# A tuned FFT-filter and MLP kernel: a last FFT stage without a turn through DRAM, and a first batch made in two copies

## The chip, the cores and the metric

The kernel runs on one core of a Trainium2 chip. The metric is the device time of one execution in microseconds (us). Each kernel was timed in rounds beside the kernel before on the same chip. The class of a result is "same" when it lies within 2%.

## The reference, cut to what matters

```python
# x: (8, 3008, 256); filt: (1505, 256); w_in: (256, 2048); w_out: (2048, 256)
X = np.fft.rfft(x, axis=1)
Y = X * (filt_r + 1j * filt_i)[None]
y = np.fft.irfft(Y, n=3008, axis=1)
t = y.reshape(24064, 256)
h = t @ w_in
out = (h * (1 / (1 + np.exp(-beta * h)))) @ w_out
```

So each of eight batches is filtered in the frequency domain along its 3008 rows, and every row then goes through an MLP with 2048 hidden values.

## The kernel before

The FFT is done as matmuls in four stages: first stage (`s1`), second and third stage with the filter product between them (`s23`), last stage (`s4`). Between the stages the data change their layout. From the second batch on that is done through DRAM: `d1` between the first and second stage, `d2` between the third and the last, and a third exchange `dy` with a transposing read, since the MLP wants channels on the partitions. A copy of a matmul's result out of the accumulators (PSUM) into SBUF, by VectorE or ScalarE, is called an eviction here. The names in the profile are `a` and `d` (or `d_931`) for the first exchange, `z`, `d` (or `d_932`) and `zz` for the second, `yo`, `dy`, `y` for the third.

The MLP goes in steps: one block of 512 rows and one slice of 128 hidden values is one step. Sixteen steps are a block, 752 steps the whole. The FFT units of later batches are put between MLP steps by a table, `plan`:

```python
def s4(b, i, on_act):                      # last stage, 16 units per batch
    ...
    nc.tensor.matmul(ps[:KP], lhsT=t4[:], rhs=s["zz"][g][:, jj : jj + 2, :], ...)  # table stationary
    evac(s["yo"][...], ps[...], on_act, inv_scale)
    if jj + 2 == JG:
        nc.sync.dma_start(s["dyr"][...], s["yo"]...)          # y to DRAM
def y_read(b):
    for c in range(NDC):
        nc.sync.dma_start_transpose(ys[b][:, c, :S], s["dy"][c, :S, :])   # and back, turned
...
place(w_, 0.00, 0.14, u1(b, True))         # batch 1 (the second): first stage at steps 0 to 13
place(w_, 0.28, 0.60, u23(b), True)
...
place(w_, 0.03, 0.48, u23(b), True)        # later batches; parts of a window of 96 steps
```

`u1(b, True)` lets every other eviction of the first stage go to ScalarE, and `True` in `place` ("clear") keeps a unit off the steps whose number modulo 16 is 0, 1, 14 or 15, where VectorE copies the output block `ost` out.

The first batch has no MLP to hide behind. Its stages run first, on chip, with transposes. There the filter's imaginary part is loaded once to 64 partitions, negated into the other 64 by GpSimd (`copy_imag`), and four rounds of transposes (`turn`) and last-stage matmuls (`last`) make all of y before the first MLP step.

## Time and profile before

The median is 845.16 us of three runs (844.58 to 845.36). I cut each execution at two points: the first MLP matmul ("start"), and the first MLP step that needs batch 1 (step 80). The rest is the time from there to the end of the span.

| kernel before, profiled run | us |
|---|---|
| span | 844.1 |
| first MLP matmul | 66.6 |
| first 80 steps | 111.5, of it TensorE busy 91.8 |
| step 80 to the end | 666.0 |
| period of a batch in the steady part | 96.26 |

The mark for step 80 is 178.09, after the waits of 4.6 us for the turned y that fall inside that step. In the other kernels the mark is that step's first matmul, so here about half a microsecond of the step's work counts with the first 80 that counts with the rest elsewhere. This is the windows view of the first 80 steps (stretch, length, busy time of PE, PEld, DVE, ACT and POOL with instruction counts, granted clock, DMA share, GB/s; PE is TensorE's matmuls, PEld its weight loads, DVE VectorE, ACT ScalarE, POOL GpSimd, SPq SyncE's queue, and the granted clock is the share of full speed that TensorE was given), and then the SyncE's issues in it (start, us, what):

```profile
66.60:178.09 111.49, 91.76 (x562) 59.07 (x573) 46.29 (x68) 72.45 (x117) 23.51 (x28) 0.91 0.66 160
```

```profile
85.99 0.30 SPq L496 DMA_DIRECT2D d_931<-a_1078  x1
91.56 0.38 SPq L507 DMA_DIRECT2D a_1131<-d_931  x1
...
132.52 0.36 SPq L554 DMA_DIRECT2D d_932<-z  x1
139.61 2.43 SPq L561 DMA_DIRECT2D zz<-d_932  x4
```

### The profile page before, as it was taken

To read this page: it belongs to the slowest core of one execution; us is meant where nothing else is said; L and a number is where in the kernel's file an instruction comes from. 1 tells how busy PE (TensorE), PEld (TensorE's weight loads), DVE (VectorE), ACT (ScalarE), POOL (GpSimd) and SP (SyncE) were. 2 spreads that over 40 slices of the span, in tenths; PEclk is the share of its full clock that TensorE was granted. 3 is DMA by queue.
4 is the path that set the end of the run, shared out by engine and by line. 5 is a ranking of instruction groups with operands and counts; after the bars stand their busy time and mean duration, and the time that the engine had idled before them with its cause. 6 is when DMAs were issued, how large, how long until landed. Compare 5 with 4: busy or idle time off the path is not lost.

```text
span 844.1 us, 14640 instructions
## 1 busy us (share of the span) xinstructions
PE 797.0 (94%) x5634; PEld 553.8 (66%) x5723; DVE 410.9 (49%) x638; ACT 602.0 (71%) x911; POOL 179.9 (21%) x189
## 2 busy tenths in 40 slices
PE   7589886979999999999999999999999999999997
PEld 4476564657666776677666876677666776666665
DVE  7643483326563575627564475636565463510101
ACT  5627576748867787678866787678866788677775
POOL 5792242013210241003310232003300131000000
PEclk9778998889999999999999999999999999999999
DMA  8574627852198134951289323961266423550101
GB/s 167 117 164 84 164 82 179 262 99 64 47 275 230 57 106 110 310 146 47 61 216 267 83 89 100 280 188 61 63 194 186 113 64 92 151 142 26 52 26 50
DMA packets 132280, 110.06 MB, mean 130 GB/s; under 512 B 47009, under 2 KB 117682, under 8 KB 132210
## 3 DMA queue, kind: packets, MB, share of 16 engines
q1 hardware_dynamic: 127570, 95.74, 39.8%
q0 software_dynamic: 4640, 13.37, 9.2%
q8 instruction: 45, 0.74, 0.4%
q14 instruction: 25, 0.20, 0.1%
HBM read 54.01 MB, written 57.67 MB: 132 GB/s over the span
## 4 chain that ended last, share of the span: by engine, by line
PE 85%; DMA 7%; issue 3%; DVE 2%; POOL 2%; SPq 1%; ACT 1%; DVEq 0%; POOLq 0%; ACTq 0%
PE acc L693 38%; PE hps L665 35%; DMA fi_sb<-in_filt_i_dram 2%; PE pz L424 1%; DVE ost L705 1%; POOL fi_sb L138 1%; DMA zz<-d_932 1%; DMA xg<-in_x_dram 1%; DMA dy<-yo 1%; DMA y<-dy 1%; DMA d_931<-a_1078 1%; DMA a_3015<-d_2714 1%; DMA a_6777<-d_6476 0%; DMA a_1131<-d_931 0%; DVE q_t L529 0%
## 5 line engine op out<-in xcount | busy, mean ns | idle before, releaser
L674 ACT ACTIVATE gT<-hps,beta_sb 128x512 bf16<-128x512 f32 x752 | 516.1, 687 | 193.4 <-PE hps L665 171.4
L693 PE MATMUL acc<-wout_sb,gT 128*128 128x256 bf16 x3008 | 457.5, 274 | 3.8
L665 PE MATMUL hps<-y,win_sb 128*128 128x512 bf16 (+7 forms) x1643 | 433.6, 353 | 5.1 <-DMA y<-dy 4.6
L693 PEld LDWEIGHTS <-gT 128*128 128x128 bf16 x3008 | 293.6, 98 | 163.3 <-issue 7.6
L535 POOL TENSOR_TENSOR v_t<-p_t,q_t 128x512 bf16<-128x512 f32 x84 | 106.5, 1268 | 407.0 <-DVE q_t L529 348.2
L665 PEld LDWEIGHTS <-win_sb 128*128 128x128 bf16 x1728 | 166.1, 98 | 28.8 <-issue 4.9
L705 DVE COPY ost<-acc 128x512 f32<-128x512 f32 x94 | 60.4, 683 | 214.5 <-PE acc L693 214.1
L113 POOL DMA_DIRECT2D xg<-in_x_dram x32 | 17.2, 537 | 101.6 <-PE ps_4036 L491 8.8
L517 PEld LDWEIGHTS <-t_102 128*128 128x128 bf16 x168 | 16.0, 98 | 19.3 <-issue 4.6
L570 PEld LDWEIGHTS <-t_101 96*96 96x96 bf16 x112 | 14.0, 126 | 21.6 <-DMA zz<-d_932 8.2
L491 PEld LDWEIGHTS <-t_100 94*96 94x96 bf16 x112 | 14.0, 125 | 13.5 <-issue 0.9
L545 PEld LDWEIGHTS <-t_103 128*128 128x128 bf16 x168 | 16.0, 98 | 8.4 <-issue 3.1
L114 POOL DMA_DIRECT2D xg<-in_x_dram x32 | 16.4, 513 | 0.0
L138 POOL TENSOR_SCALAR fi_sb<-fi_sb 64x1536 f32<-64x1536 f32 x4 | 16.3, 4100 | 0.1
L395 PE MATMUL psz<-t3q,qb_t 128*128 128x128 bf16 x48 | 7.9, 244 | 8.3 <-DVE qb_t L386 7.7
L184 PE MATMUL pw<-wz 128*128 128x512 bf16 x37 | 14.2, 477 | 1.2 <-DVE wz L178 1.2
L149 POOL TENSOR_SCALAR wout_sb<-ws,rbeta_sb 128x256 bf16<-128x256 f32 x16 | 14.5, 940 | 1.3 <-DMA ws<-in_moe_w_out_dram 1.3
L99 ACT ACTIVATE z_t<-psz 128x512 bf16<-128x512 f32 x12 | 7.1, 597 | 8.8 <-PE psz L395 8.7
L395 PEld LDWEIGHTS <-qb_t 128*128 128x128 bf16 x48 | 5.1, 110 | 10.3 <-DVE qb_t L386 10.1
L424 PE MATMUL pz<-ident,z_t 128*96 128x128 bf16 x64 | 11.2, 353 | 0.5 <-ACT z_t L99 0.5
L424 PEld LDWEIGHTS <-z_t 128*96 128x96 bf16 x64 | 10.8, 257 | 0.8 <-ACT z_t L99 0.8
L101 DVE COPY zz<-pz 96x1024 bf16<-96x1024 bf16 x8 | 5.5, 687 | 9.8 <-PE pz L424 9.8
(1026 smaller groups left out, 661.3 us busy)
## 6 DMA issues: line engine op xcount, KB each, us to landing
out_dram<-ost SPq DMA_DIRECT2D x47, 512.0 KB, 3.0
dy<-yo SPq DMA_DIRECT2D x28, 384.0 KB, 5.0
xg<-in_x_dram POOLq DMA_DIRECT2D x32, 320.0 KB, 6.5
ws<-in_moe_w_out_dram SPq DMA_DIRECT2D x4, 512.0 KB, 6.6
xg<-in_x_dram POOLq DMA_DIRECT2D x32, 56.0 KB, 6.7
fr_sb<-in_filt_r_dram SPq DMA_DIRECT2D x8, 192.0 KB, 6.7
fi_sb<-in_filt_i_dram SPq DMA_DIRECT2D x8, 192.0 KB, 7.3
d_932<-z SPq DMA_DIRECT2D x4, 384.0 KB, 3.8
```

The lines of the kernel that those rows point to most:

```text
L113: nc.gpsimd.dma_start(t[:80], xv[:80, js, :])
L114: nc.gpsimd.dma_start(t[80:NP], xv[80:NP, js, :])
L138: eng.tensor_scalar_mul(fi_sb[M:P, ks_, :], fi_sb[:M, ks_, :], -1.0)
L149: nc.gpsimd.tensor_scalar_mul(wout_sb[:, f0 + i, :], ws[:, i, :], rbeta_sb[:, f0 + i : f0 + i + 1])
L424: nc.tensor.transpose(pz[:KP, e, dc * P : (dc + 1) * P], z_t[:, dc, :, JG * g + 4 * i + e], ident[:],)
L517: nc.tensor.matmul(ps[:, e, :], lhsT=t2[:, k0 + e, :, :].rearrange("p c k -> p (c k)"), rhs=s["a2"][g][:, kk + e, :], start=True, stop=True,)
L535: nc.gpsimd.tensor_tensor(v_t[:], p_t[:], q_t[:], ALU.add)
L545: nc.tensor.matmul(ps[:, e, :], lhsT=t3[:, k0 + e, :, :].rearrange("p c k -> p (c k)"), rhs=v_t[:, e, :], start=True, stop=True,)
L665: nc.tensor.matmul(hps[:, pos - t0 : pos - t0 + ln], lhsT=win_sb[:, dc, fb * P : (fb + 1) * P], rhs=ys[b][:, dc, n0 : n0 + ln], start=(dc ...
L674: nc.scalar.activation(gT[:, :tn], hps[:, :tn], ACT.Silu, scale=beta_sb[:, fb : fb + 1])
L693: nc.tensor.matmul(acc[tb // 2][:, tb % 2, :], lhsT=gT[:, tb * P : (tb + 1) * P], rhs=wout_sb[:, fb, :], start=(fb == 0 and tb % 2 == 0), ...
L705: nc.vector.tensor_copy(ost[:, 2 * h : 2 * h + n, :], acc[h][:, :n, :])
```

## The change

Its intent is threefold. The last stage takes the data as the stationary side in all batches, so that y comes out with channels on the partitions and needs no third exchange. The first batch's spectrum is made twice, with the filters loaded to both halves of the partitions, so that no negation and no copies stand in the start (the later batches still need the negated filter; GpSimd makes it after the start, from 66 us on). And of the first batch's last stage only the first of four classes of rows is made before the MLP; three are placed within the first 50 steps, in a row order that `store` undoes.

The core of the diff, cut (`...`):

```diff
 def s4(b, i, on_act):
-    nc.tensor.matmul(ps[:KP], lhsT=t4[:], rhs=s["zz"][g][:, jj : jj + 2, :], ...)
-    ...
-            nc.sync.dma_start(s["dyr"][...], s["yo"]...)
-def y_read(b):
-    ...
+    last4(s["zz"][g], t4, jj, dc, yv[:, :, 4 * jq : 4 * jq + 4], on_act)
+def last4(zz, tab, jj, dc, dst, on_act):
+    for e in range(4):
+        nc.tensor.matmul(ps[:, e, :NP], lhsT=zz[:, jj + e, dc * P : (dc + 1) * P], rhs=tab[:], ...)
+    evac(dst, ps[:, :, :NP].rearrange("p j n -> p n j"), on_act, inv_scale)
...
 for g in range(NG):
-    load_filters(g)
+    load_filters(g, 0, nc.sync)
+    load_filters(g, M, nc.gpsimd)
...
+    for h in range(WI):
+        nc.gpsimd.dma_start(win_sb[:, :, fs], ...)
...
+    gp.tensor_scalar(keep[:], ...)        # the mask, now behind the transfers above
...
-    for g in range(NK // KG): copy_imag(g, nc.gpsimd)
...
+    place(1, 13, uz(1), per=1)            # classes 1 to 3 of the first batch, in the MLP
+    place(14, 30, uz(2), per=1)
+    place(31, 50, uz(3), per=2)
-    place(w_, 0.00, 0.14, u1(b, True))
-    place(w_, 0.28, 0.60, u23(b), True)
-    place(w_, 0.61, 0.71, u1(b + 1, True), per=2)
-    place(w_, 0.03, 0.48, u23(b), True)
+    place(16, 30, u1(1), per=2)
+    place(41, 63, u23(1), True, per=2)
+    place(50, 70, u1(2), per=3)
+    place(a + 3, a + 47, u23(b), True)
```

## The prediction

> **What bounds the kernel now.** I read the page's busy shares first, then the chain that ended last in order of time, then windows cut at the events of that chain.
>
> ```profile
> PE 797.0 (94%) x5634; PEld 553.8 (66%) x5723; DVE 410.9 (49%) x638; ACT 602.0 (71%) x911; POOL 179.9 (21%) x189
> ```
>
> TensorE bounds the whole. Each of the 752 MLP steps (one block of 512 tokens, one 128-slice of the hidden layer) streams 2 x 512 + 4 x 256 columns; the chain shows the pair and the four at 0.85 us together. The windows show where even TensorE is not kept busy (stretch, its length, PE busy, PEld, DVE, ACT, POOL, granted clock, DMA share, GB/s):
>
> ```profile
> 66.60:84.30 17.70, 17.43 (x96) 10.52 (x98) 5.24 (x8) 13.53 (x23) 3.13 (x6) 0.88 0.58 100
> 139.60:147.60 8.00, 0.31 (x2) 0.00 (x0) 0.00 (x0) 0.96 (x2) 0.76 (x2) 0.68 1.04 225
> 160.00:178.00 18.00, 13.22 (x89) 8.69 (x90) 1.58 (x3) 10.59 (x17) 0.00 (x0) 0.96 0.93 219
> ...
> 229.73:325.99 96.26, 95.55 (x679) 66.62 (x688) 54.20 (x82) 71.61 (x108) 19.33 (x20) 1.00 0.53 148
> ```
>
> From 230 us the period of one batch (96 steps plus the FFT of a later batch) is 96.26 us with TensorE 99% busy: nothing but TensorE work can shorten it. Everything idle lies before 178 us. The chain there:
>
> ```profile
> 14.20 7.23 DMA fi_sb<-in_filt_i_dram
> 21.44 8.09 DMA fi_sb<-in_filt_i_dram
> ...
> 34.93 4.09 POOL fi_sb L138
> ...
> 49.12 5.51 PE pz L424 x32
> ...
> 66.60 1.01 PE hps L665 x2
> ...
> 85.99 5.50 DMA d_931<-a_1078
> ...
> 139.61 7.97 DMA zz<-d_932
> ...
> 162.08 6.63 DMA dy<-yo
> 168.76 3.04 SPq L589
> 171.87 5.97 DMA y<-dy
> 178.09 0.85 PE acc L693 x4
> ```
>
> So: the first MLP matmul at 66.6 us, after filter loads, a negation of the filter on GpSimd and four rounds of transposes; then 80 steps until batch 1 is wanted, which last to 178 us and wait for the first exchange through DRAM, the second, and the third, which turns y. The DMA view of 21 to 31 us shows how the filters load:
>
> ```profile
> GB/s 225 242 176 152 168 184 213 283 217 213 197 123 209 172 254 238 209 225 160 143 221 160 213 193 184 188 152 168 188 307 369 311 369 332 365 352 332 348 152 49
> ```
>
> About 190 to 200 GB/s for filter pieces (32 partitions each), 330 to 370 once the 128-partition load of w_out is alone.
>
> [...] here a 94x128 load takes 97 ns and a 96x96 one 126 ns[...] the granted clock is 0.50 at 30 to 35 and 55 to 65 us.
>
> **Part 1: last stage data-stationary.** Per batch 16 matmuls of 512 columns (16 x 0.2133 = 3.41 us) become 64 of 94 columns, each with its own weight load of 128 columns. In the set-up the same form (psa, 96 columns) went 8 in 0.34 us, 42.5 ns each at full clock, so the load hides: 64 x 0.042 = 2.7 us. Saved: 0.7 us of TensorE a batch, in six steady batches 4.4 us. The write of y to DRAM and the turning read vanish; in the steady part they were hidden. VectorE's evictions stay 16, 0.53 us each. The new row order swaps which side of d1 and d2 has 512-byte pieces; hidden.
>
> **Part 2: time to the first MLP matmul.** Removed: the four GpSimd negations (4 x 4.1 us, between 27 and 45 us) and four ScalarE copies (4 x 1.48) from this path, and three quarters of the transposes and last-stage work. Before, those four rounds took 49.1 to 66.6 = 17.5 us. Now one class: 16 transposes with a contiguous operand, about 0.1 us each against 0.172, two VectorE evictions of 0.69, four last-stage units with 0.53 us evictions, alternating engines: about 3.5 us. So 14 us saved here.
>
> Added: the filters are loaded twice, 6.2 MB instead of 3.1, the copy to partitions 64 to 127 from GpSimd's queue, with w_in (2.1 MB) behind it. The built order of the changed kernel shows one more thing. [...] The tiny `keep` mask, which the first filter product on VectorE needs, now stands behind the four w_in transfers, and the last of these waits for the third of the four filter groups. So the whole product loop starts only then. Before, a group of 0.77 MB took 4.1 us from about 13 us. A doubled group of 1.57 MB takes 7.85 us at an estimated 200 GB/s [...], 4.7 us if both halves run at 330. The third group lands at 36.6 or 27; with 2.5 us for the last transfer and the mask, products start at 39 or 29.5.
>
> The loop: 12 rounds of 2 VectorE products at 0.6 us, 14.4 us, if TensorE keeps up. It has 4 instead of 2 matmuls of 256 columns, 8 of 128 and up to 6 transposes, about 1.3 us at full clock, 1.7 to 2.3 at half; it wakes cold as it did at 32 us (1.7 us a round for two rounds). I take 19 us in all with the last eviction. z is ready at 58 or 48.5 (before: 49.1), the first MLP matmul at 61.5 or 52. I lean to the slow side and take 59.5: a gain of 7 us.
>
> **Part 3: the first 80 steps.** Before: 66.6 to 178 = 111.3 us. TensorE's work was 80 x 0.853 + 3.4 + 5.1 + 3.4 + 3.4 (stages of batch 1, first stage of batch 2) = 83.6; so 27.7 us are waits and low clock. After: 68.3 + 3.4 + 5.1 + 2.7 + 3.4, and three classes at 16 x 0.08 + 16 x 0.042 = 1.95, in sum 88.8. The waits:
> - half clock at the start and small change: 5 us;
> - steps 50 to 59 hold 9 units of stages 2 and 3 (3 x 0.69 us on VectorE each), 8 evictions of the first stage at 0.69, now all on VectorE, an output block 1.4: 26 us on VectorE against 14 on TensorE. Before, steps 34 to 44 had 18 against 12.8 and lost 3.6. Estimate 8.5;
> - z's last write now leaves at step 66 and its read is wanted at step 71. Before, the write left at 132.5 us and the data were there at 147.6: 15 us. Five steps with three first-stage units are 5 us: about 9 us lost, as before 8.
> - the turning exchange (162 to 178 us, about 7 us of idle) is gone; the read for batch 2 comes only 6 steps ahead: 1 us.
>
> Sum 88.8 + 23.5 = 112: what the third exchange gave back, the extra work and the tighter placing use up. Gain 0, within 6 us either way.
>
> **Sum.** 845.2 - 7 - 0.7 - 4.4 = 833; I take 831, since the placing looks tuned and my waits may be too large.
>
> **Rivals.**
> - The two halves of the SBUF load in parallel: products from 29.5 us, total about 823. For it: the 330 to 370 GB/s of a 128-partition load shows that the engines have the rate. [...]
> - The duplicate costs more than the negation: software-queued pieces of 1 KB load slower than the others, w_in lands late; the first MLP matmul stays at 66 us and only part 1 counts: about 840. For it: the share of the DMA was already 0.86 to 1.1 between 5 and 30 us.
> - The waits of part 3 are smaller than I count and the class pipeline saves the turning exchange outright: 10 us more, about 821. For it: TensorE had 7 us idle just there. Against: VectorE's 26 us in ten steps.
> - Small matmuls with weight loads run at 80 ns, as the old last stage in the set-up did at half clock: 64 x 0.08 = 5.1 us, a loss of 1.7 us a batch, about 847.
>
> **Range.** The first-matmul time spans 52 to 66, part 3 is good to 6 us either way, part 1 to 3; together about 12 us: 818 to 843. The 2% mark is 828.3, a little below my figure: faster 0.38, same 0.60, slower 0.02.
>
> **What would show it.** Right: first MLP matmul at 58 to 62 us; VectorE waiting on GpSimd's mask before its first filter product; step period of a batch 95.5 us; a VectorE-bound stretch and a wait on zz before 175 us. Wrong: filter products running from 20 us, a rate above 300 GB/s from 12 to 30 us, or a period above 96.3 us.

## The result, and the profile after

The changed kernel took 837.38 us (836.01 to 841.72, five runs) beside 845.16 for the kernel before (843.19 to 845.63, five runs). The ratio is 0.9916, 95% interval 0.989 to 0.9943: the class is "same", the time is inside the predicted range and 6 us above the predicted 831.

| profiled run | before | after | difference |
|---|---|---|---|
| first MLP matmul | 66.6 | 51.6 | -15.0 |
| first 80 steps | 111.5 | 118.0 | +6.5 |
| step 80 to the end | 666.0 | 670.3 | +4.3 |
| span | 844.1 | 839.9 | -4.2 |

This profile fell on the longest of the five executions, 841.72; I come back to that with a second profile below. The page's line of busy shares:

```profile
PE 784.3 (93%) x5975; PEld 552.2 (66%) x6071; DVE 410.9 (49%) x670; ACT 585.7 (70%) x885; POOL 185.6 (22%) x200
```

TensorE was busy for 12.7 us less than before (784.3 against 797.0), and the span shrank by 4. The chain that ended last shows the early part (start, us, what):

```profile
15.55 17.22 DMA fi_sb<-in_filt_i_dram
...
32.79 10.36 DMA fi_sb<-in_filt_i_dram
...
47.70 1.95 PE pz L481 x16
...
51.56 1.08 PE hps L709 x2
...
87.73 8.33 DMA d<-a
96.14 3.55 DMA a<-d
...
145.54 7.62 DMA d<-z
153.22 4.15 DMA zz<-d
157.41 0.81 PE ps L489 x8
```

Gone from the chain are the negation on GpSimd, the 32 transposes in a row at 49 us, and at the end the exchange of `dy`. What the reader should compare are the two lines with `a`: the last write of batch 1's first exchange left at 85.99 before and leaves at 87.73 now, though the MLP begins 15 us sooner. The last write of the second exchange leaves 13 us later than before, 145.54 against 132.52. The 15 us were won at the start and did not reach the transfers that gate step 80.

The windows view of the first 80 steps and of one steady period:

```profile
51.56:169.56 118.00, 97.42 (x698) 64.73 (x712) 69.47 (x110) 61.42 (x93) 51.47 (x49) 0.91 0.58 142
202.28:299.56 97.28, 95.16 (x726) 67.28 (x737) 51.88 (x81) 71.82 (x109) 19.39 (x20) 1.00 0.41 114
```

In the first 80 steps VectorE is busy for 69.5 us instead of 46.3: the first-stage evictions of batches 1 and 2 and the last-stage evictions of batch 1 all go to it now (half of each went to ScalarE), and so do those of the three classes. TensorE is busy for 5.7 us more (97.4 against 91.8) and idle for about as long as before (20.6 against 19.7): the waits for the transfers are 12.5 us instead of 16.1, and others took their place. And the steady period got longer, 97.28 against 96.26, although TensorE's busy time in it fell: TensorE now idles 2.1 us in every period, where it idled 0.7.

In TensorE's timeline two waits stand out (start, us, instruction, and in brackets the idle time and its releaser):

```profile
157.41 0.81 PE L489 MATMUL ps<-t,zz 96*128 96x94 bf16 x8 [10.10 <-DMA zz<-d]
304.46 0.38 PE L584 MATMUL ps<-v_t,t 128*128 128x256 bf16 x2 [1.29 <-POOL v_t L574]
```

### The profile page after: what moved, and what is told of

Same layout as the page of the kernel before. A ratio compares the mean times of both kernels' runs of the same rounds, so it can differ in the third digit from the quotient of the medians. Undisturbed runs are those within 1.5% of the kernel's fastest.

```text
span 839.9 us, 15300 instructions
## 1 busy us (share of the span) xinstructions
PE 784.3 (93%) x5975; PEld 552.2 (66%) x6071; DVE 410.9 (49%) x670; ACT 585.7 (70%) x885; POOL 185.6 (22%) x200
## 4 chain that ended last, share of the span: by engine, by line
PE 82%; DMA 8%; DVE 5%; issue 3%; POOL 1%; ACT 0%; SPq 0%; DVEq 0%; POOLq 0%
PE acc L737 38%; PE hps L709 34%; DMA fi_sb<-in_filt_i_dram 3%; PE ps L489 3%; PE ps L532 3%; DVE ost L749 2%; PE ps L556 2%; PE ps L584 2%; DVE q_t L568 1%; POOL v_t L574 1%; DMA d<-a 1%; DVE p_t L566 1%; DMA d<-z 1%; DMA mark<-xg 1%; DMA xg<-in_x_dram 1%
## 5 line engine op out<-in xcount | busy, mean ns | idle before, releaser
L568 DVE TENSOR_TENSOR q_t<-ps,fi_sb 64x512 f32<-64x512 f32 x168 | 115.7, 689 | 2.3
L107 DVE CAST a<-ps 96x512 bf16<-96x512 f32 x112 | 76.5, 686 | 68.9 <-PE ps L532 68.6
L109 DVE TENSOR_SCALAR y<-ps 128x376 bf16<-128x376 f32 x126 | 68.4, 548 | 79.2 <-PE ps L489 78.9
L566 DVE TENSOR_TENSOR p_t<-ps,fr_sb 128x512 f32<-128x512 f32 x84 | 58.1, 692 | 48.1 <-PE ps L556 46.7
L489 PEld LDWEIGHTS <-zz 96*128 96x128 bf16 x512 | 35.9, 101 | 39.2 <-DMA zz<-d 10.6
L105 ACT ACTIVATE z<-ps 128x512 bf16<-128x512 f32 x84 | 49.5, 590 | 11.8 <-PE ps L584 11.7
L489 PE MATMUL ps<-t,zz 96*128 96x94 bf16 x448 | 36.6, 208 | 10.9 <-DMA zz<-d 10.1
L532 PE MATMUL ps<-xg,t 94*96 94x512 bf16 x112 | 42.7, 383 | 2.9 <-ACT z L105 1.4
L584 PE MATMUL ps<-v_t,t 128*128 128x256 bf16 x168 | 32.1, 273 | 11.4 <-POOL v_t L574 8.4
L556 PE MATMUL ps<-a,t 128*128 128x256 bf16 x168 | 32.3, 274 | 3.5 <-DMA a<-d 2.4
L584 PEld LDWEIGHTS <-t 128*128 128x128 bf16 x168 | 15.2, 97 | 19.6 <-issue 9.3
```

The source lines that it names most:

```text
L107: nc.vector.tensor_copy(dst, src)
L109: nc.vector.tensor_scalar_mul(dst, src, scale)
L489: nc.tensor.matmul(ps[:, e, :NP], lhsT=zz[:, jj + e, dc * P : (dc + 1) * P], rhs=tab[:], start=True, stop=True,)
L532: nc.tensor.matmul(ps[:KP], lhsT=t1[:], rhs=s["x"][g][:, jj : jj + 2, :], start=True, stop=True)
L556: nc.tensor.matmul(ps[:, e, :], lhsT=t2[:, k0 + e, 1:3, :].rearrange("p c k -> p (c k)"), rhs=s["a2"][g][:, kk + e, :], start=True, stop=True,
L566: nc.vector.tensor_tensor(p_t[:], ps[:], fr_sb[:, k0 : k0 + 2, :], ALU.mult)
```

## The experiments

All outputs are right. Medians are quoted; the kernel before had 843.53, 845.51 and 843.80, each on another chip, so small differences are read from the marks of the profiles.

### Part 1 alone

The kernel before with only the new last stage: `s4` as in the change, no `dy`, placing as before.

```diff
-        nc.tensor.matmul(ps[:KP], lhsT=t4[:], rhs=s["zz"][g][:, jj : jj + 2, :], ...)
+        for e in range(4):
+            nc.tensor.matmul(ps[:, e, :NP], lhsT=s["zz"][g][:, jj + e, dc * P : (dc + 1) * P], rhs=t4[:, :NP], ...)
...
-        for c in range(NDC):
-            nc.sync.dma_start_transpose(ys[b][:, c, :S], s["dy"][c, :S, :])
```

> The kernel before with part 1 alone: the last stage of batches 1 to 7 data-stationary, straight into y, no write and turning read. Theory: the 64 small matmuls of a batch take 2.7 us against 3.4, so the steady period falls from 96.26 to 95.5 us, and the wait for the turning exchange before 178 us (about 7 us) goes: 833 us. Rival (weight loads are not hidden, 80 ns a pair): the period rises to about 98 us and the total is 845 or more. Second rival (the period of 97.28 us seen after the change comes from the small matmuls): the period here is about 97.3 us.

It took 832.17 us (831.57 to 832.30), ratio 0.9861 (0.9847 to 0.9876): 11.4 us less than before, and 5 us less than the whole change. Windows of the first 80 steps and of a period:

```profile
66.36:170.91 104.55, 90.17 (x604) 59.98 (x616) 45.18 (x68) 71.03 (x117) 23.58 (x29) 0.92 0.56 141
220.46:315.83 95.37, 94.67 (x726) 67.31 (x736) 52.07 (x82) 71.75 (x108) 19.33 (x20) 1.00 0.41 116
```

The start is where it was, the first 80 steps lose 6.9 us (the wait of 4.6 us for the turned y is gone), the rest loses 7.4, the period is 95.37. The prediction's 95.5 for part 1 was right; it was another part of the change that made it 97.28. It also follows that parts 2 and 3, with their new placing, cost 5 us more than they bring, in spite of their 15 us at the start. The next run shows that the steady spacing is more than the whole of it: with the spacing put back they bring 3 us.

### The steady products spaced as before

The changed kernel with one range of the placing set back to the fractions of before, 0.03 and 0.48 of 96 steps:

```diff
-        last_at = a
+        last_at = int(a)
-        place(a + 3, a + 47, u23(b), True)
+        place(a + 2.88, a + 46.08, u23(b), True)
```

> The changed kernel with the steady placing of stages 2 and 3 put back to the fractions of before (unit 9 again at step 109 of the first steady batch instead of 114, so no three units in a row behind the output copies). Theory: the longer period of 97.28 us is the VectorE bunch; it falls to about 95.5 us in six batches, total 837.4 - 6 x 1.78 = 826.7 us. Rival (the small matmuls or the DMA layout lengthen the period): the period stays at 97.3 us and the total at 837.

It took 828.97 us (828.40 to 829.50), ratio 0.9824 (0.9807 to 0.9840), 8.4 us less than the changed kernel. The windows view of a period, and the chain of the changed kernel at the place that differs:

```profile
216.60:312.19 95.59, 94.78 (x726) 67.37 (x736) 51.87 (x82) 71.71 (x108) 19.40 (x20) 1.00 0.42 116
```

```profile
299.56 0.89 DVE ost L749 x2
...
302.28 0.70 DVE q_t L568
...
303.14 1.27 POOL v_t L574
304.42 0.04 issue
304.46 0.38 PE ps L584 x2
```

The busy times are the same and the period is 1.7 us shorter. The cause can be worked out from the rule in `place`. With a = 80, the ninth of the 14 units falls on 83 + 8 x 44/13 = 110.08 in the changed kernel, so step 110, which is 14 modulo 16; "clear" moves it to 114, and the next two follow at 115 and 116. Before it fell on 82.88 + 8 x 43.2/13 = 109.46, step 109, and stayed. Three units in a row behind the output copies are what VectorE then owes at one time (before, these units stood at 109, 114 and 116), and the matmul of the third stage waits for the sum on GpSimd. Since 96 is a multiple of 16 this recurs in every batch. From step 80 to the end this kernel takes 660.2 us instead of 670.3.

### The mask early

The changed kernel with the mask `keep` computed before GpSimd's transfers.

```diff
+    gp.tensor_scalar(keep[:], m_p[:], ...)      # and the two lines after it
     for g in range(NG):
         load_filters(g, 0, nc.sync)
         load_filters(g, M, nc.gpsimd)
...
-    gp.tensor_scalar(keep[:], m_p[:], ...)
```

> The changed kernel with the mask computed before the filter and w_in transfers are issued on GpSimd. Theory: the filter products start at about 20 us instead of 28.7, but they still end on the last filter group from the other queue, which landed at 43.2 us; first MLP matmul stays at 50 to 52 us, total 836 to 838. Rival (the mask is what sets the first MLP matmul): the loop ends 9 us earlier, first MLP matmul at about 43 us, total 828.

It took 837.04 us (835.77 to 837.44), ratio 0.9918. First VectorE's timeline of the changed kernel, then of this run, with the first products and the last wait:

```profile
28.66 0.48 DVE L403 SCALAR_TENSOR_TENSOR qb_t<-ps2q,keep,fi_sb 128x256 bf16<-128x256 f32 x1 [8.37 <-POOL keep L232]
...
43.27 0.69 DVE L408 TENSOR_TENSOR qb_t<-ps2q,fi_sb 128x512 bf16<-128x512 f32 x1 [1.28 <-DMA fi_sb<-in_filt_i_dram]
```

```profile
23.47 0.48 DVE L403 SCALAR_TENSOR_TENSOR qb_t<-ps2q,keep,fi_sb 128x256 bf16<-128x256 f32 x1 [3.47 <-DMA fi_sb<-in_filt_i_dram]
...
42.91 0.69 DVE L408 TENSOR_TENSOR qb_t<-ps2q,fi_sb 128x512 bf16<-128x512 f32 x1 [1.31 <-DMA fi_sb<-in_filt_i_dram]
```

The products behind the mask start 5.2 us sooner, at 23.5 and not at the 20 expected, since they now wait for a filter piece. The last wait among them, for a late filter piece, ends at 42.9 instead of 43.3. The wait of 8.37 us for the mask was real and worth nothing: it lay in front of a later wait.

### w_in behind the filters

The run above, and GpSimd's four transfers of w_in issued after two tiny copies that need the last filter pieces.

```diff
+    tie = small("tie")
+    gp.tensor_copy(tie[:], fi_sb[:, NK - 1, :1])
+    gp.tensor_copy(tie[:], fr_sb[:, NK - 1, :1])
+    for h in range(WI):
+        nc.gpsimd.dma_start(win_sb[:, :, fs], ...)
```

> As the run with the early mask, and the w_in transfers wait until the last filter pieces have landed. Theory: w_in took DMA time between 24 and 40 us ahead of the last filter group of the other queue; without it the filters are in at about 36 us, the first MLP matmul at about 46 us, total about 832. Rival 1 (w_in is not what delays them): last filter at 43 us, no change, 837. Rival 2 (w_in or w_out then comes too late): first MLP matmul at 50 us or later, or waits on win_sb and wout_sb in the first steps, 837 to 840.

The first MLP matmul came at 45.99, as expected. The time was 837.45 us (835.61 to 837.89), no better than the run above; the expected 832 was missed. The first 80 steps took 118.9 us against 114.0 there, so all of the 5.2 us was given back before step 80. The chain says how far it held:

```profile
80.26 9.46 DMA d<-a
89.80 3.60 DMA a<-d
...
140.25 8.27 DMA d<-z
148.59 4.06 DMA zz<-d
152.69 0.81 PE ps L492 x8
```

In the run above these transfers start at 86.75, 94.25, 141.65 and 149.74. The lead is 6.5 us at the last write of the first exchange, 4.4 at its read, and 1.4 at the last write of the second. The granted clock was 0.79 from 94 to 106 us here, after TensorE had waited for the exchange, and 1.00 in the same place of the run above (98 to 107); 12 x 0.21, about 2.5 us of the loss, is an estimate of what comes from that. The wait before it was 3.6 us here and 1.3 us there; the section on the changed kernel's second profile comes back to this.

### All classes before the MLP

The changed kernel with the three classes moved out of the MLP.

```diff
+    for g in range(1, NJG):
+        for i in range(2):
+            turn_z(g, i)
+        for i in range(2 * NDC):
+            last_z(g - 1, i, i % 2 == 1)
...
-    place(1, 13, uz(1), per=1)
-    place(14, 30, uz(2), per=1)
-    place(31, 50, uz(3), per=2)
```

> The changed kernel with all four classes of the first batch's last stage before the MLP instead of one. Each of the three classes moved costs the start two groups of transposes and twelve small matmuls at half clock, 1.95 + 1.27 us in the changed kernel, and takes some 0.9 + 0.5 us of full-clock TensorE work out of the first 80 steps. Theory (TensorE is not what bounds the first 80 steps, the exchanges and VectorE are, so taking the classes out of them gains little): first MLP matmul near 61 (from 51.6), first 80 steps 114 to 117 us (from 118), time 842 to 846. Rival A (the classes inside the MLP are what lengthened the first 80 steps from 111.5 to 118): first 80 steps 111, time 837 to 840. Rival B (nothing of the start reaches the end, as when the start came 5 us earlier with w_in late): time 837.

It took 839.86 us (838.95 to 841.34), ratio 0.9940 (0.9918 to 0.9962). The start was 57.40, so three classes cost 5.8 us there and not ten, and the first 80 steps took 110.7. The numbers are those of rival A, and the theory's are missed. The time is not told apart from the changed kernel's own ratio of 0.9916 and, later, 0.9942. So in the changed kernel what the start wins by leaving the three classes to the MLP, the MLP loses.

### Only the first 80 steps replaced

The changed kernel with other places for batch 1 and batch 2 in the first 80 steps.

```diff
-        place(16, 30, u1(1), per=2)
-        place(37, 37, [lambda: a2_read(1)], per=9)
-        place(41, 63, u23(1), True, per=2)
-        place(68, 68, [lambda: zz_read(1)], per=9)
+        place(12, 26, u1(1, True), per=2)
+        place(33, 33, [lambda: a2_read(1)], per=9)
+        place(36, 58, u23(1), True)
+        place(65, 65, [lambda: zz_read(1)], per=9)
-        place(50, 70, u1(2), per=3)
+        place(54, 68, u1(2, True), per=2)
```

> The changed kernel with only the placing within the first 80 steps changed: the second batch's first stage at steps 12 to 26 (was 16 to 30), its read at 33 (37), its products spread over steps 36 to 58 one at a time (were bunched at 41 to 63, several to a step), its last read at 65 (68), the third batch's first stage at 54 to 68 and clear of them. Steady part as in the changed kernel. Theory (the first 80 steps are bound by the two exchanges through DRAM and by the VectorE bunch between them, not by TensorE): first 80 steps 106 to 110 us instead of 118, the last TensorE wait for the read under 5 us instead of 10.1, time 826 to 830. Rival A (the bunch is bound by its own chain, product after transform, so placing doesn't move it): within 2 us of 837.4. Rival B (the earlier first stage waits for its input load, 4 us or more on TensorE): 833 to 838.

It took 829.65 us (828.85 to 831.42), ratio 0.9821 (0.9803 to 0.9840). The window, and the SyncE's issues:

```profile
51.66:159.27 107.61, 93.73 (x712) 62.85 (x712) 59.08 (x94) 68.38 (x109) 52.62 (x50) 0.97 0.61 146
```

```profile
74.83 7.75 SPq L537 DMA_DIRECT2D d<-a  x3
93.13 1.77 SPq L546 DMA_DIRECT2D a<-d  x4
...
132.08 0.33 SPq L589 DMA_DIRECT2D d<-z  x1
139.62 6.61 SPq L596 DMA_DIRECT2D zz<-d  x4
```

The theory held: the first 80 steps took 10.4 us less than in the changed kernel's first profile. The last write of the second exchange leaves at 132.08 instead of 145.54. About 10 us of first-stage evictions went from VectorE to ScalarE (69.5 to 59.1 us busy; 61.4 to 68.4), and the products go one to a step (by the table, two fell on each of steps 51 and 52; five of them still share a step with a first-stage unit). TensorE's wait for `zz` fell from 10.1 to 3.7 us in two pieces, while its wait for `a` rose from 2.4 to 5.3. Neither rival showed: placing did move the bunch, and no wait for the input load appears. From step 80 on, the time is 670.3 us as in the changed kernel. Which of the edits, the earlier first stage, the even products or the alternating evictions, brings how much was not separated.

### All at once

The kernel with w_in behind the filters, with the placing of the first 80 steps just shown and with the even spacing of the steady part.

> The changed kernel with all at once: the mask computed before GpSimd's transfers, the w_in transfers behind the last filter pieces (first MLP matmul at 46.0 there), the first 80 steps placed as in the run of that alone, and the steady products spaced evenly as in the run of that alone (period 95.6, total 828.97). Theory (the start's 5 us were given back in the exchanges of the first 80 steps, and those are shorter here): the gains of the even spacing (8.4) and of the first window (about 9) add, and 2 to 5 us of the earlier start remain: 814 to 820, period 95.5. Rival (the gains of the first window and of the even spacing are the same VectorE time, counted twice): 824 to 829.

It took 811.27 us (810.65 to 811.63), ratio 0.9600 (0.9586 to 0.9615). This beats both kernels, by 34 and by about 27 us. Windows of the first 80 steps and of a period:

```profile
45.67:149.60 103.93, 94.28 (x713) 63.17 (x713) 59.08 (x94) 68.29 (x109) 54.80 (x52) 0.97 0.66 156
216.35:311.94 95.59, 95.41 (x738) 67.36 (x736) 51.89 (x82) 71.75 (x108) 19.36 (x21) 1.00 0.43 117
```

The rival is out. The theory held and was too cautious, 811 against 814 to 820: the gains add, and the first 80 steps are moreover shorter here than with the placing alone (103.9 against 107.6). The start of 45.7, worth nothing in the run with w_in behind the filters, now reaches the end. Against part 1 alone the start is 20.7 us earlier and the span is 19.6 us shorter. That is what parts 2 and 3, with the two repairs of the start, are worth when the placing passes it on.

### Both filter copies on one queue

The run with w_in behind the filters, but SyncE issues both copies of the filters.

```diff
-        load_filters(g, M, nc.gpsimd)
+        load_filters(g, M, nc.sync)
```

> The run with mask early and w_in late, but both copies of the filters issued on SyncE's queue, none on GpSimd's. It measures the disputed rate. Theory (two queues in two halves of the partitions is what carried 246 GB/s where one queue carried 190 to 200 in the kernel before): the filters move at 190 to 210 GB/s and the last lands near 46 to 50, first MLP matmul 52 to 56 instead of 46.0. Rival (one queue carries 245 GB/s as well once both halves of the partitions are written, and the 190 to 200 of before came from writing only partitions 0 to 63): first MLP matmul 45 to 48.

838.47 us, the first MLP matmul at 51.66. First the last filter piece in the chain of this run, then, in the kernel with all at once, the first tie copy, which waits for the last pieces:

```profile
34.76 8.15 DMA fi_sb<-in_filt_i_dram
```

```profile
38.40 0.18 POOL L450 COPY tie<-fi_sb 128x1 f32<-128x1 f32 x1 [12.99 <-DMA fi_sb<-in_filt_i_dram]
```

The last filter piece lands at 42.91, and all filters are 16 x 2 transfers of 192 KB, so 6.29 MB from 10.6 us on: 195 GB/s. The same 6.29 MB in two queues had landed at 38.4 in the kernel with all at once: 227 GB/s counted from 10.67 us, 16% more, though two of GpSimd's sixteen pieces were issued before that. In stretches in which almost nothing but filter pieces moved, one execution each, the DMA view has 261 GB/s from two queues (11 to 29 us), 222 from one (11 to 34 us), and 209 in the kernel before, one queue and only the lower 64 partitions (12 to 27 us). The rate is within the theory's 190 to 210; the landing came sooner than its 46 to 50 and the start, 51.7, just below its 52 to 56. The rival's 45 to 48 is out. One thing isn't separated: on one queue the sixteenth piece is issued at 20.42, when the eighth has landed (13.15 + 7.25), so the two kernels may also differ in how many transfers were under way at a time. The rate from two queues agrees with what the first profile showed: the DMA view of 11 to 45 us in the changed kernel, w_in included.

```profile
DMA packets 5083, 8.37 MB, mean 246 GB/s; under 512 B 615, under 2 KB 4194, under 8 KB 5080
```

### All at once, but all classes before the MLP

Edit as in the run of that name above, on the kernel with all at once.

> The kernel with all at once (811.27 in its own call, first MLP matmul at 45.67, first 80 steps 103.93), but with all four classes of the first batch's last stage before the MLP. It asks what the four classes within the MLP are worth once the placing is right. The start grows by the 5.8 us that the same move cost the changed kernel (57.40 against 51.56). Theory (the first 80 steps are now within 10 us of their TensorE work, 94.3 of 103.9 us, so taking out the three classes' 6.7 us of TensorE work shortens them): 98 to 101 for the first 80 steps, time 811 to 814. Rival (the first 80 steps still end on the exchanges through DRAM, so they stay at 102 to 104): time 815 to 817.

It took 819.64 us (817.85 to 822.96), ratio 0.9718 (0.9685 to 0.9751).

```profile
54.22:157.70 103.48, 87.97 (x604) 57.95 (x615) 49.19 (x77) 67.91 (x110) 47.01 (x41) 0.97 0.61 143
```

The first 80 steps take 103.5 us though TensorE has 6.3 and VectorE 9.9 us less to do in them than in the kernel with all at once. TensorE's waits for `a` and `zz` grew from 4.9 to 10.3 us, which takes up most of what it was spared. So here these 80 steps are set by the exchanges and by where their units stand, and the rival's 102 to 104 is right; the theory's 98 to 101 is not. The start came at 54.2, later than the 51.5 expected, and of these 8.6 us the span shows 8.1. With a good placing the classes within the MLP are worth 8 us, where in the changed kernel they were worth about nothing.

### The changed kernel again

No edit.

> The changed kernel itself, once more, for a second profile: the first one fell on its longest execution (841.72 against 836.0 to 837.7 of the others), and its first 80 steps took 118.0 us, where the run with only the mask early took 114.0 with the same placing. Theory (the 118.0 belong to that execution, with a granted clock of 0.91 in the stretch against 0.94): time 836 to 838, first 80 steps 112 to 115 us, steady period again 97.28. Rival (118 is the changed kernel's own, and the mask early saved 4 us of it): first 80 steps 117 to 119.

It took 838.95 us (837.84 to 840.26), ratio 0.9942 (0.9922 to 0.9961). The first MLP matmul was at 50.43, the first 80 steps took 117.7, the rest 670.4, the period was 97.27. The rival is right in so far as 118 us was no accident of one execution. I don't take the 4 us of the run with the mask early (114.0) for a gain of that edit, though: its time is within 0.4 us of the changed kernel's first median, and the run with w_in behind the filters, which has the early mask too, took 118.9. What makes these 80 steps vary between 114 and 119 us is not settled by an experiment, but the six profiles with this placing fall in two groups. Where TensorE's wait for `a` was 1.3 to 1.5 us (mask early, even spacing, one queue), the granted clock in the 4 us after it was 1.00 and the 80 steps took 114.0 to 115.1. Where that wait was 2.4 to 3.6 us (both profiles of the changed kernel, w_in behind the filters), the clock there was 0.50 to 0.74 and they took 117.7 to 118.9.

### The marks of all profiled runs

| kernel | start | first 80 steps | rest | span | median |
|---|---|---|---|---|---|
| before | 66.6 | 111.5 | 666.0 | 844.1 | 845.16 |
| changed | 51.6 | 118.0 | 670.3 | 839.9 | 837.38 |
| changed, again | 50.4 | 117.7 | 670.4 | 838.5 | 838.95 |
| part 1 alone | 66.4 | 104.6 | 658.6 | 829.5 | 832.17 |
| even spacing | 52.2 | 115.1 | 660.2 | 827.5 | 828.97 |
| mask early | 51.2 | 114.0 | 670.3 | 835.5 | 837.04 |
| w_in behind filters | 46.0 | 118.9 | 670.4 | 835.3 | 837.45 |
| classes first | 57.4 | 110.7 | 670.4 | 838.5 | 839.86 |
| first 80 steps replaced | 51.7 | 107.6 | 670.3 | 829.6 | 829.65 |
| all at once | 45.7 | 103.9 | 660.3 | 809.9 | 811.27 |
| all at once, classes first | 54.2 | 103.5 | 660.3 | 818.0 | 819.64 |
| one queue | 51.7 | 114.7 | 670.1 | 836.5 | 838.47 (one run) |

The rest has three values only, by the last stage and by the spacing of the products: 666 for the old last stage, 659 to 660 for the new one, 670 for the new one with the bunch.

## Why the prediction was right or wrong

The class, the range and the rough time were right, the time in part by luck. The sum behind them was not right: three terms were off, by -8, +6 and +9 us, and of these errors 7 us were left over. The sizes below are those of the profiled spans, which fell by 4.2 and in the second profile by 5.6; the prediction's terms summed to about 12. (The 0.7 us of batch 1's last stage is in that sum twice, once by itself and once in the 112 us of the first 80 steps.)

**Part 1, last stage.** The step holds. The small matmuls run eight in 0.33 to 0.34 us, 42 ns each, so the rival of 80 ns falls; the period was foreseen at 95.5 and is 95.37 when part 1 stands alone. From step 80 on part 1 alone gave 7.4 us where 4.4 were foreseen; 2.1 us of it lie between step 80 and the first steady period, where the granted clock was 0.95 after the wait for the turned y, and 1.00 without that wait.

**The period of the changed kernel.** "Period of a batch 95.5 us" failed for it: 97.28, which the prediction itself had named as a sign of being wrong. The prediction treated the steady placing as unchanged. The step missed is a rounding, 2.88 and 46.08 made 3 and 47: one unit falls on step 110, is pushed to 114 and makes a bunch of three on VectorE. Shown by the even spacing: 10 us back from step 80 on. The term was -4.4 and was measured as +4.3.

**Part 2, the start.** The mechanism of the term was half right. VectorE did wait on the mask, as foreseen, 8.4 us: in the trace of the changed kernel GpSimd's later issues of filter pieces wait for earlier ones, 0.3 to 1.6 us each, its last issue of w_in 0.9 us for a filter piece, and the mask behind them came at 28.4 us. But the mask did not gate the loop's end, which the run with the mask early shows; the last filter pieces did. The rate was mis-sized: 200 GB/s was the estimate, beside 190 to 200 for the filter pieces of the kernel before, and 227 to 246 were measured. So the products behind the mask started at 28.7 and not at 39 (one product, which needs no mask, ran at 19.6), and the first MLP matmul came at 51.6 instead of 59.5: the term was -7 and measured -15. The rival with both halves at the full 330 GB/s is not true either; it had the start at 52 for the wrong reason. The prediction's two readings of the granted clock differ in what TensorE had to do: 0.50 at 30 to 35 us came after it had been busy for 0.8 of 5 us, and at 55 to 65 us the clock was 0.50 too, with TensorE busy for 9.2 of 10 us.

**Part 3, the first 80 steps.** Its list of waits was right in kind: a stretch bound by VectorE and, after it, a wait for `zz`, 9 us foreseen and 10.1 found. The 1 us foreseen for the read of batch 2 isn't in the trace; a wait of 2.4 us (3.4 in the second profile) for the read of batch 1's `a`, which the list had not, is. The sum of 112 was 6 too small: the added TensorE work was right (5.2 us foreseen, 5.7 more busy time found), but waits and low clock, which should have fallen from 27.7 to 23.5, came to 29.2. The prediction gave the total of TensorE work and waits, but did not follow the chain of batch 1 against the clock. The first stage now stands 16 steps later behind the start (GpSimd issues that batch's input load at 51.6 us, before at 44.6), and its 16 evictions are VectorE's alone. So the last write of the first exchange leaves 36.2 us after the start instead of 19.4, which takes up the 15 us won, and the second leaves later than before. That placing and evictions decide is shown by the run with only the first 80 steps replaced (-10 us), and that, once they are good, it is not TensorE's or VectorE's total by the two kernels whose 80 steps took 103.5 and 103.9 with 6 and 10 us of difference in those. In the changed kernel itself the total still counted: without the three classes its 80 steps were 7 us shorter. What each edit of the placing brings stays open.

**The rivals.** "The waits of part 3 are smaller" was wrong for the changed kernel. But its remark that there is idle time at the turning exchange was right: part 1 alone shortened the first 80 steps by 6.9 us, 5.4 of it idle time. The prediction's own line shows 4.8 us of idle there (18.00 less 13.22), not 7.

## What to carry to other kernels

When work is taken off the start of a pipelined kernel, follow one chain of the next batch against the clock, from load to last read: if its first transfer does not move, the gain at the start is spent on waiting. A table of places tuned in fractions should not be rounded without looking at what the rounding does to the rules on top of it; here the rounding cost 8 us in all, as much as the whole change saved. And a long wait in a trace, like the one for the mask, is worth removing only if nothing behind it waits for something later.
